# RWKV attention feeding a dense block: a shorter first block, own terms as TensorE products, idle products only in planned gaps

## The chip, the cores and the metric

One core of one Trainium2 chip. The metric is device time in microseconds (us). Kernels that are compared were run in turn on the same chip, together with the kernel before; the experiments ran in groups on chips 1, 4 and 8, so across groups the ratios are compared and not the medians. A kernel on one core has no second core to show a slow die; every profiled run quoted here was classed as fast (one unprofiled run of e5_kw_after_rT was slow). A run's time is about 1.7 us longer than its profiled span (640.26 against 638.5 in the changed kernel).

Short names: PE is TensorE (matmul), DVE is VectorE, ACT is ScalarE, POOL is GpSimd, SP is the engine that issues the loads.

## The reference, cut to what matters

```python
# r, k, v: (4, 8, 768, 48); w, u: (8, 48)
for t in range(S):
    cur = einsum('bhd,bhe->bhde', u * kt, vt)            # the "own term" of step t
    y[:, :, t] = einsum('bhd,bhde->bhe', rt, state + cur)
    state = w * state + einsum('bhd,bhe->bhde', kt, vt)
x = y.transpose(0, 2, 1, 3).reshape(B * S, H * D)        # (3072, 384)
h = x @ w_in                                             # (3072, 2048)
return (h - tanh(h)) @ w_out                             # (3072, 384)
```

## The kernel before

The attention works in 24 units of 64 steps of two batches. Within a unit the decay is taken out by scaling: r times powers of w, k times inverse powers, so that the step-by-step recurrence becomes matmuls ("levels", "outputs", "state"). Sixteen units come early, 8 later. The dense block turns finished units (two make one block x transposed, tile `xt`) into h, g and o; its weights arrive as 64-bit words in 16 pieces and are converted by five DVE and two ACT instructions each.

The kernel does not write its instructions in a fixed order. It adds tasks with an engine, an estimated cost and predecessors to a plan, and a list scheduler puts them in an order for each engine. The chip then runs each engine's queue in that order, so an instruction that waits holds up everything behind it (a case of 4.34 us is shown below).

```python
IDLE = 80
...
    def turn_over():                                    # one pair of idle products
        for i in range(2):
            T.matmul(idle[:, 0, :128], ident, ident, start=True, stop=True)
    kept = [add("PE", .25, turn_over, due=2e9) for _ in range(IDLE)]
...
    # unit n (early: n < 16)
        def own():
            t.rk = work.tile([128, H, D], F32, name="rk", tag="rk")
            E.tensor_tensor(t.rk, rt[:, :, :D], t.kt, ALU.mult)         # r*k
        def own_sum():
            t.du = work.tile([128, H], F32, name="du", tag="du")
            V.tensor_reduce(t.du, t.rk, axis=mybir.AxisListType.X, op=ALU.add)
        def diagonal(hs):                                               # onto the diagonal
            ...
            A.mul(t.at[:, h % 2, h // 2], same, t.du[:, h : h + 1])
...
        x.turn = add("PE", .46, lambda: turn(rt), [x.r, ..., tabs, downs, flagged])
        x.rT = add("DVE", .62, scale_r, [x.turn, ups])
        x.kw = add(e, cost, lambda: E.tensor_tensor(kw[:, :, :D], t.kt, w_down, ALU.mult), [x.k, downs, b2.out])
        turn_k = add("PE", .46, lambda: turn(kw), [x.kw, x.rT])
        x.kT = add("ACT", .5, copy_k, [turn_k])
        x.rk = add(e, cost, own, [x.r, x.k, b2.du, b1.rk])
        now = add(e, cost, lambda: E.tensor_tensor(t.rk, t.rk, ub, ALU.mult), [x.rk, bonus])
        x.du = add("DVE", .47, own_sum, [now, b2.diag])
        ...
        x.lev = add("PE", ..., levels, [x.kT, x.rT] + ...)
        x.cp = add("DVE", .64, lambda: V.copy_predicated(t.at, before, lev), [x.lev, x.diag])
        x.out = add("PE", 1.3, outputs, [x.cp, x.v, b1.xt, b1.rest, b1.add])
...
    for t in plan.order():
        t.run()
```

## Time and profile before

| | before |
|---|---|
| time, median of the first three runs | 646.72 us (644.96 to 647.88) |
| span of the profiled run | 646.0 us |
| PE busy | 624.5 us (97%) |
| first h product of the dense block | 54.38 us in the chain, 54.31 in PE's timeline |
| idle products (identity times identity) | 160 |

The prediction shows the lines for the idle products, the chain and the stages. Three more rows are needed to compare with later. The span is cut into 40 slices of 16 us; each digit is the busy share in tenths (for PEclk the granted clock, for DMA the busy share of the transfer engines).

```profile
DVE  3558899999996755757656555555645555454552
PEclk9999999999999999999999999999999999999998
DMA  6957549676101001001113110100103100100101
```

The reader is to see that the clock never drops, and that the transfers have free room between 32 and 96 us (5, 7, 5, 4). The same for 30 to 90 us in one row (columns: stretch, length, busy time of PE, weight loads, DVE, ACT, POOL with counts; granted clock; DMA share; GB/s):

```profile
30.00:90.00 60.00, 54.79 (x934) 46.38 (x926) 48.37 (x80) 36.07 (x89) 18.71 (x24) 1.00 0.60 131
```

### The profile page before, as it was taken

The page shows a single profiled execution, that of the slowest core. Times are in us where ns is not written, and L with a number is a line of the kernel's source. Part 1 is how long each engine was busy: PE and PEld are TensorE (multiplying, and loading weights), DVE is VectorE, ACT ScalarE, POOL GpSimd, SP SyncE. Part 2 cuts the span into 40 slices and gives each one's busy share as a digit, 9 for nine tenths or more (in the row PEclk, how much of TensorE's full clock was granted, in tenths as well). Part 3 has the DMA queues.
Part 4 walks back from the last instruction along what each step waited for, and adds up shares of the span by engine and source line. Part 5 has one row for each costly group of instructions (what it writes and reads, how often), then busy time and mean ns, then how long its engine had stood idle before and what let it go on. Part 6 is the DMA issues. An engine that isn't in the chain of part 4 may idle for free.

```text
span 646.0 us, 13413 instructions
## 1 busy us (share of the span) xinstructions
PE 624.5 (97%) x5383; PEld 471.8 (73%) x5383; DVE 420.3 (65%) x659; ACT 375.4 (58%) x788; POOL 113.1 (18%) x145
## 2 busy tenths in 40 slices
PE   9999899999999999999999999999999999999995
PEld 8997676776777777777777777777776776776773
DVE  3558899999996755757656555555645555454552
ACT  1436678877976545545556545655545655654752
POOL 1032243326021102103102100210116203001000
PEclk9999999999999999999999999999999999999998
DMA  6957549676101001001113110100103100100101
GB/s 131 210 98 177 125 86 151 164 133 161 25 14 30 15 1 26 12 1 35 34 31 80 26 25 1 38 18 1 37 10 60 38 2 8 26 0 9 25 0 29
DMA packets 88163, 33.80 MB, mean 52 GB/s; under 512 B 78620, under 2 KB 82972, under 8 KB 88092
## 3 DMA queue, kind: packets, MB, share of 16 engines
q1 hardware_dynamic: 85788, 31.67, 24.0%
q0 software_dynamic: 2304, 1.18, 0.7%
q8 instruction: 44, 0.72, 0.5%
q14 instruction: 27, 0.22, 0.1%
HBM read 26.94 MB, written 4.72 MB: 49 GB/s over the span
## 4 chain that ended last, share of the span: by engine, by line
PE 83%; DVE 10%; DMA 2%; issue 2%; ACT 1%; POOL 0%; DVEq 0%; ACTq 0%; SPq 0%; POOLq 0%
PE o L199 35%; PE h L162 35%; PE h L386 6%; PE yk_ps L444 4%; PE x_ps L485 2%; DMA rt<-in_r_dram 1%; DVE g L192 1%; DMA kt<-in_k_dram 1%; DVE power L136 1%; PE x_ps L444 1%; DVE tg L188 1%; DVE g L186 1%; DVE tg L190 1%; DVE at L587 1%; DVE w_in_sb L137 1%
## 5 line engine op out<-in xcount | busy, mean ns | idle before, releaser
L199 PE MATMUL o<-w_out_sb,g 128*128 128x384 f32 x768 | 281.2, 490 | 6.0 <-DVE g L192 6.0
L162 PE MATMUL h<-xt,w_in_sb 128*128 128x256 f32 x1152 | 280.9, 381 | 0.0
L162 PEld LDWEIGHTS h<-xt,w_in_sb 128*128 128x128 f32 x1152 | 216.4, 190 | 62.5 <-issue 0.2
L199 PEld LDWEIGHTS o<-w_out_sb,g 128*128 128x128 f32 x768 | 141.9, 190 | 70.2 <-DVE g L192 9.0
L171 ACT ACTIVATE s<-h 128x512 f32<-128x512 f32 x96 | 57.3, 597 | 176.2 <-PE h L162 176.1
L188 DVE SCALAR_TENSOR_TENSOR tg<-s,tg 128x512 f32<-128x512 f32 x96 | 68.9, 718 | 117.0 <-ACT tg L175 117.0
L186 DVE TENSOR_TENSOR g<-h,th 128x512 f32<-128x512 f32 x96 | 65.5, 682 | 35.3 <-ACT tg L175 34.9
L192 DVE COPY_PREDICATED g<-small,tg 128x512 f32<-128x512 int32 x96 | 74.2, 772 | 7.9 <-DVE g L186 0.5
L190 DVE SCALAR_TENSOR_TENSOR tg<-q,tg 128x512 f32<-128x512 f32 x96 | 70.7, 736 | 6.0
L179 ACT ACTIVATE small<-s,smallb 128x512 f32<-128x512 f32 x96 | 70.3, 732 | 0.0
L177 ACT ACTIVATE q<-s,m1b 128x512 f32<-128x512 f32 x96 | 69.6, 725 | 0.0
L173 ACT ACTIVATE th<-h 128x512 f32<-128x512 f32 x96 | 57.4, 598 | 1.5 <-PE h L162 1.5
L175 ACT ACTIVATE tg<-h 128x512 f32<-128x512 f32 x96 | 57.1, 595 | 0.0
L592 POOL TENSOR_TENSOR state<-state,power 128x384 f32<-128x384 f32 x22 | 36.8, 1672 | 94.0 <-DVE state L570 64.6
L564 POOL DMA_DIRECT2D xt<-rest x72 | 36.9, 518 | 92.0 <-ACT rest L550 54.2
L386 PE MATMUL h<-ident 128*128 128x128 f32 x320 | 41.1, 289 | 2.7 <-POOL ident masks.py:199 1.5
L577 POOL TENSOR_TENSOR kw<-kt,w_down 128x384 f32<-128x384 f32 x8 | 9.1, 1139 | 192.5 <-PE yk_ps L444 192.5
L508 ACT ACTIVATE at<-same,du 128x64 f32<-128x64 f32 x128 | 33.9, 340 | 14.5 <-DVE du L501 14.4
L386 PEld LDWEIGHTS h<-ident 128*128 128x128 f32 x320 | 39.4, 203 | 3.0 <-POOL ident masks.py:199 1.5
L497 POOL TENSOR_TENSOR rk<-rt,kt 128x384 f32<-128x384 f32 x8 | 8.4, 1051 | 97.8 <-DMA rt<-in_r_dram 87.9
L587 DVE COPY_PREDICATED at<-before,x_ps 128x512 f32<-128x512 int32 x23 | 16.6, 721 | 10.8 <-PE x_ps L444 10.7
L444 PEld LDWEIGHTS yk_ps<-at,vt 64*64 64x64 f32 x768 | 13.4, 134 | 13.6 <-DVE at L587 8.2
(88 smaller groups left out, 427.3 us busy)
## 6 DMA issues: line engine op xcount, KB each, us to landing
st<-in_moe_w_out_dram SPq DMA_DIRECT2D x8, 768.0 KB, 5.2
rt<-in_r_dram SPq DMA_DIRECT2D x48, 96.0 KB, 3.2
kt<-in_k_dram SPq DMA_DIRECT2D x48, 96.0 KB, 3.3
vt<-in_v_dram SPq DMA_DIRECT2D x48, 96.0 KB, 3.2
st<-in_moe_w_in_dram SPq DMA_DIRECT2D x16, 288.0 KB, 5.6
out_dram<-part SPq DMA_DIRECT2D x24, 96.0 KB, 2.2
out_dram<-o SPq DMA_DIRECT2D x24, 96.0 KB, 2.2
st<-in_moe_w_in_dram SPq DMA_DIRECT2D x16, 96.0 KB, 5.3
```

What stands on the lines that cost most here:

```text
L162: self.nc.tensor.matmul(t.h2[:, z], self.w_in_sb[:, t.f // 2, kk, z * 128 : (z + 1) * 128], self.xts[t.j][:, kk].rearrange("p b t -> p (b ...
L171: A.activation(out, t.h, AF.Square)
L173: A.activation(out, t.h, AF.Tanh)
L175: A.activation(out, t.h, AF.Tanh, scale=G1)
L177: A.activation(out, t.s, AF.Square, bias=self.m1b)
L179: A.activation(out, t.s, AF.Relu, bias=self.smallb, scale=-1.0)
L186: V.tensor_tensor(t.g, t.h, t.th, ALU.subtract)
L188: V.scalar_tensor_tensor(t.tg, t.s, C4, t.tg, ALU.mult, ALU.mult)
L190: V.scalar_tensor_tensor(t.tg, t.q, K1, t.tg, ALU.add, ALU.mult)
L192: V.copy_predicated(t.g, t.small.bitcast(I32), t.tg)
L199: self.nc.tensor.matmul(self.outs[i], t.g2[:, z, i * C : (i + 1) * C], self.w_out_sb[:, t.f + z, :], start=t.first and z == 0, stop=t.last ...
L386: T.matmul(idle[:, 0, :128], ident, ident, start=True, stop=True)
```

## The change

Three intentions:

1. The first two units ("direct") turn the raw keys as soon as they land and scale them afterwards by the transposed table, so that nothing waits for the table's way back; their part of `xt` is written without the small fills by DMA.
2. For 8 units, the own terms (sum over d of r·u·k) are computed as a second set of small TensorE products whose diagonal is copied out, instead of DVE's product, product with u, and sum.
3. Idle products are no longer a fixed 80 pairs: the plan puts one in for each 0.18 us of planned PE idle time, until the first h product.

Smaller parts of the change were never tested alone. For the 8 units the decay of the state moves from POOL to ACT, and the first two state copies move from DVE to ACT. The plan gets start times for the engines and other transfer costs: a weight piece counted 768 x 1024 bytes at 230e3 bytes per us, 3.42 us, and now counts 2.5 us.

Core of the diff (cut; memory for the new tiles, the moved state work and the final checks are left out):

```diff
+OWN = 8
-IDLE = 80
...
-    kept = [add("PE", .25, turn_over, due=2e9) for _ in range(IDLE)]
+    plan.fill = "PE", .18, lambda: T.matmul(idle, ident, ident, start=True, stop=True)
...  (in the scheduler)
+            if filling and t.engine == self.fill[0]:
+                for i in range(int((start - free[t.engine]) / self.fill[1])):
+                    done.append(SimpleNamespace(..., run=self.fill[2]))
+                filling = t is not self.fill_until
...  (weight pieces: the plan's transfer cost)
-        of = [add("SP", .55, step, [free], data=weights.COLS * 1024 / len(weights.piece(n)[1]))
+        of = [add("SP", .55, step, [free], data=2.5 / len(weights.piece(n)[1])) for _ in weights.piece(n)[1]]
...
+        early, product = n < L * (FIRST + 2), n < OWN
+        direct = j == 0
...
+        if direct:
+            own_rs = add("ACT", .5, own_r, [x.turn])
+            x.rk = add("PE", .46, lambda: turn(t.kt, x_banks[n == 1][:, :, :256]), [x.k])
+            own_ks = add("ACT", 1.1, lambda: own_k(x_banks[n == 1][:, :, :256], u_col), [x.rk, keeps])
+            x.kT = add("DVE", .62, scale_k, [x.rk, doubled])
+        else:
+            now = add("PE", .46, lambda: turn(kw), [x.kw, x.rT])
+            x.kT = add("ACT", .5, copy_k, [now])
+            own_rs = x.rT
+            if product:
+                own_ks = add("ACT", 1.1, lambda: own_k(turned, w_u), [now, w_us])
+        if product:
+            x.own = add("PE", .7, own_levels, [own_rs, own_ks, x.rT, x.kT])
+            x.diag = add("DVE", .64, lambda: V.copy_predicated(t.at, same..., own_lev), [x.own, b2.out])
+        else:                                            # as before: rk, times u, sum, diagonal
...
-        x.cp = add("DVE", .64, lambda: V.copy_predicated(t.at, before, lev), [x.lev, x.diag])
+        x.cp = add("DVE", .64, lambda: V.copy_predicated(t.at, before, lev), [x.lev, b2.out] + ([] if product else [x.diag]))
```

## The prediction

> **What bounds the kernel now.** I read the page first: TensorE (PE) is busy for 97% of the span. What it is busy with shows in the costliest groups (columns: line, engine, operation, tiles, shapes, count | busy us, mean ns of one | idle time before and its releaser).
>
> ```profile
> PE 624.5 (97%) x5383; PEld 471.8 (73%) x5383; DVE 420.3 (65%) x659; ACT 375.4 (58%) x788; POOL 113.1 (18%) x145
> ...
> L199 PE MATMUL o<-w_out_sb,g 128*128 128x384 f32 x768 | 281.2, 490 | 6.0 <-DVE g L192 6.0
> L162 PE MATMUL h<-xt,w_in_sb 128*128 128x256 f32 x1152 | 280.9, 381 | 0.0
> ...
> L386 PE MATMUL h<-ident 128*128 128x128 f32 x320 | 41.1, 289 | 2.7 <-POOL ident masks.py:199 1.5 <-issue 1.2
> ```
>
> The reader is to see the last line: 320 records of identity times identity, 160 idle products (two records each), whose result nobody reads. Next, the chain of work that ended last, limited to the first 60 us (start, us, what):
>
> ```profile
> 1.53 8.71 PE h L386 x52
> 10.23 0.15 PE x_ps L391
> 10.38 7.79 PE h L386 x68
> 18.17 0.44 PE x_ps L379 x4
> ...
> 31.66 1.17 issue
> ...
> 35.85 3.32 PE h L386 x28
> 39.17 0.44 PE x_ps L485 x4
> 39.61 3.13 PE h L386 x28
> ...
> 48.38 4.02 PE h L386 x36
> ...
> 54.38 2.79 PE h L162 x12
> ```
>
> The idle products ARE the chain. Added up in this view they take 39.8 us of the 52.9 us between 1.53 and 54.38, where the first real h product (L162) starts; the useful PE work in between is 11.9 us and the one wait 1.17 us. They were planned at 0.25 us a pair, and 68 records (34 products) take 7.79 us: 0.229 us each, 0.46 us a pair. So 80 pairs planned as 20 us of filler became nearly twice that, in an engine that runs its orders in sequence.
>
> Last, the busy time by stretch (stretch, length, then busy time with counts of PE, PEld, DVE, ACT, POOL; clock; DMA share; GB/s):
>
> ```profile
> 0.00:52.00 52.00, 49.31 (x673) 47.99 (x674) 27.13 (x57) 17.38 (x49) 8.52 (x28) 1.00 0.72 146
> 52.00:100.00 48.00, 43.61 (x718) 33.93 (x717) 42.94 (x72) 36.31 (x90) 14.53 (x17) 1.00 0.63 133
> 100.00:150.00 50.00, 45.48 (x736) 32.96 (x738) 48.47 (x78) 39.04 (x90) 19.24 (x23) 1.00 0.79 148
> 150.00:200.00 50.00, 49.40 (x375) 37.47 (x365) 49.17 (x78) 38.58 (x80) 9.83 (x4) 1.00 0.18 49
> 200.00:300.00 100.00, 100.00 (x691) 73.62 (x691) 64.57 (x99) 57.97 (x118) 17.76 (x23) 1.00 0.10 19
> ```
>
> Three stages: to 52 us PE turns idle products while VectorE (DVE) has 25 us free; from 52 to 200 us DVE is full (weight conversion, dense elementwise work, attention units) and PE loses 9.5 us; from 200 us PE alone is full. Whatever the start saves passes to the end only if DVE and the DMA can follow through the middle stage.
>
> **What the Trainium skill says.** (1) "TensorE: Matmul & The Clock Gate", Part 1: the PE array runs at half clock until about 3.4 us of sustained work, and falls back after an idle window of that size. The trace agrees at the start: the first 16 records fill 3.47 us (217 ns each), later ones need 115 ns, and the change comes near 7 us. This is why idle products exist, and why the 16 first ones that remain will be slow. (2) "FP8 and Floating Point Precision", TensorE Precision Notes: true FP32 takes four passes. An estimate from it and the 2.4 GHz of the first page: 4 x 128 / 2.4 = 213 ns; the trace has 229. So 0.18 us, the new planning cost of one idle product, is still too short. (3) "TensorEngine Tiling (Array Packing)", 64x64 Mode: four independent tiles. The trace agrees: 16 such products (32 records, x_ps<-rT,kT) take 0.62 us in the chain, 0.04 us each, so own terms by products are cheap. (4) "DMA: Bandwidth & Descriptors", Specifications: line rate wants at least 512 B per transfer. Here 78620 of 88163 packets are smaller, and from 10 to 15 us the DMA share is 0.98 at only 190 GB/s. The start is near this limit.
>
> **The change part by part.** I counted instructions in the order of the changed program, engine by engine.
>
> *Idle products*: 160 become 49 (groups of 16, 6, 4, 7, 3, 3, 3, 7), all ahead of the first h. The first 16 are cold: about 25 records by 7 us, the remaining 7 at 0.115, so they end near 7.8 us (6.3 us). The other 33 at 0.229 cost 7.6. Sum 13.9 instead of 39.8: 25.9 us less.
>
> *First block*: the raw keys are transposed as soon as they land and scaled afterwards by the table, so that turning does not wait for the table's way back. I walk the chain with durations of the trace. Decay column on PE 7.8 to 8.0; clamp 0.43, scan 0.70, reciprocal 1.78 on DVE to about 11.1; scaled r (0.69), doubled table 0.41, scaled k 0.69 to about 13.4; own products and levels of unit 0 on PE to 14.6; DVE has bounds, one weight step (0.55) and two predicated copies (0.74 each) to about 16.1; outputs, transpose and state products to 18.0. Unit 1 runs through DVE behind this: k, two kw, r, the two copies, to 21.6; outputs to 23; ACT copies xt and k of unit 2 to 24.1; state and level products to 25.7. Beside it the conversion of weight piece 0 ends on DVE at about 26. So the first h starts at about 26.5 us, against 54.4. The other check: 1.5 us start, 13.9 idle, 10.4 useful on PE add up to 25.8. The direct units leave out the little fills of xt by DMA; those were beside other work already.
>
> But this is not 28 us of gain. At its first h the old kernel had more units behind it: 11.9 us of useful work against 10.4, of which some is new.
>
> *Own terms of 8 units*: PE gains 16 products per unit, 0.57 us each time: 4.6 us, plus 0.5 us for the extra thirds in the two direct units. This lies on PE, the bound of the late stage: a sure cost of 5.1 us. DVE loses three steps of 0.47 (product, times u, sum) and gains one copy of 0.63: 0.78 x 8 = 6.2 less. With two k scalings (+1.2) and two state copies moved to ACT (-0.9) DVE is 5.9 us lighter. ACT loses 8 small scalings (2.12 us per unit, as four take 1.06) and gains 4 scalings of k (about 1.3) and 4 of the state decay (about 1.2, off POOL): even.
>
> **The sum.** Useful PE work before: 646.0 - 39.8 idle - 2.7 start - 9.5 gaps to 200 us - 1.7 later gaps - 7.7 tail = 584.6. After: 584.6 + 5.1 = 589.7, plus 13.9 idle, 1.5 start, and if gaps and tail stay as they are (18.9): 624.0. Independently by DVE: before, DVE had done 163.5 us when its full stage ended near 195 us. After: 163.5 - 5.9 = 157.6, starting at 8.1 without a pause: 165.7, plus the share of gaps of the old full stage (4.4 in 135, here about 5) makes 171; the end moves by 24, to 623. Both roads agree. As denser work in three engines should lose a little more, I say 625.
>
> **Rivals.** (a) *DVE takes over as the bound*: 97 to 98% busy from 100 to 200 us speaks for it. In-order queues with PE, DVE and DMA all nearly full could leave DVE 8% idle instead of 3%: 12 us instead of 5, end near 631. Against it: the change itself takes 5.9 us off DVE. (b) *DMA becomes the bound*: by 160 us the DMA share adds up to 112 us; pressed into 137 us that is 82%, and the weights' 4 and the units' 3 buffers must hide the bursts. The old trace already has rt and kt landings of 5 to 7 us on the chain between 98 and 111 us. For the first h it is enough: three units and two pieces are 3.3 MB, some 20 us at 170 GB/s. A burst that holds up PE for 3.4 us would cost cold products too. That would give 632 to 638. (c) *The idle time was hidden*: had PE waited for data anyway, without fills it would wait as long and the time would be 646 + 5 = 651. Against it: in 0 to 52 us the chain shows no wait but 1.17, and DVE was waiting for PE transposes, not for data. (d) *Better than the sum*: with POOL off DVE's way and an accurate plan, half of the middle gaps vanish: 618.
>
> **Range and chances.** The saved 25.9 and the added 5.1 are nearly sure: 20.8 net. The rest is waits: 5 us fewer (d) to 11 more (a, b). Hence 625, range 616 to 636. Two per cent is 633.8; rivals (a) and (b) together reach beyond it about one time in eight. Faster 0.86, same 0.13, slower 0.01.
>
> **What would show it right or wrong.** Right: about 98 idle records with 14 us in the chain; the first h at 25 to 29 us; x_ps<-rT,kU (and rU,kU) groups near 0.6 us per unit; DVE near full from 9 us; PE full from about 172 us; the last 450 us unchanged. Wrong in the walk: a first h past 32 us, with DMA of st, kt or rt ahead of it in the chain. Wrong in the sum: PE gaps between 27 and 172 us well over 10 us, released by DVE at or g (rival a) or by DMA (rival b). A time above 640 would mean that the idle products had covered waits for data after all.

## The result, and the profile after

The changed kernel is correct and takes 638.88 us (median of 4 runs, 636.95 to 640.49) against 645.91 us of the kernel before in the same rounds. Ratios here are the mean time of one kernel's fast runs over the mean of the other's fast runs of the same rounds, so not quite the ratio of the medians: 0.9886, with a 95% interval of 0.9842 to 0.9929. That is 7 us faster and counts as "same" at the 2% line; 625 was predicted, with a range up to 636.

The page of the changed kernel, in the rows shown of before:

```profile
span 638.5 us, 13477 instructions
...
PE 609.5 (95%) x5449; PEld 452.9 (71%) x5449; DVE 416.5 (65%) x644; ACT 377.2 (59%) x789; POOL 92.8 (15%) x139
...
DVE  4796898999976766756666655455636655553651
PEclk9997999999999999999999999999999999999998
DMA  7989965782001001002113110200112100100101
```

The slices show at once what differs: the idle products' time is gone (PE 624.5 to 609.5 us busy), but the DMA digits are 8 and 9 from 16 to 80 us, and the clock drops to 7 in the fourth slice, where it was full before.

The chain of waits is no help for this profile: it breaks off at the last activation. So the first block is read from PE's timeline (start us, us, engine, line, operation, out<-in, shapes, count, and in brackets the idle time before with its releaser). First its idle products, then its own terms, then the first h:

```profile
1.53 5.42 PE L400 MATMUL h<-ident 128*128 128x128 f32 x32 [1.53 <-POOL ident masks.py:199]
...
13.25 0.70 PE L460 MATMUL x_ps<-rU,kU 48*64 48x64 f32 x32 [0.21 <-DVE kT L512]
...
27.84 0.48 PE L162 MATMUL h<-xt,w_in_sb 128*128 128x256 f32 x1
```

And the idle products in the costliest groups (busy us, mean ns of one, idle before):

```profile
L400 PE MATMUL h<-ident 128*128 128x128 f32 x98 | 14.3, 303 | 1.5 <-POOL ident masks.py:199 1.5
```

All of this is as predicted: 98 idle records, the first h at 27.84 us (26.5 said; 54.31 before), own products of 32 small matmuls in 0.6 to 0.7 us. The stages, with the edges of the prediction's table:

```profile
0.00:52.00 52.00, 43.75 (x950) 37.82 (x951) 40.09 (x73) 30.65 (x74) 8.65 (x33) 1.00 0.89 166
52.00:100.00 48.00, 41.46 (x654) 30.67 (x653) 37.14 (x62) 33.14 (x86) 5.75 (x12) 0.89 0.85 163
100.00:150.00 50.00, 46.85 (x727) 34.93 (x726) 49.43 (x77) 38.67 (x84) 12.31 (x16) 1.00 0.66 134
150.00:200.00 50.00, 48.54 (x310) 35.93 (x309) 42.84 (x68) 36.78 (x80) 4.36 (x3) 1.00 0.06 11
200.00:300.00 100.00, 100.00 (x635) 73.79 (x634) 65.30 (x98) 57.24 (x116) 18.17 (x23) 1.00 0.10 19
```

Up to 52 us PE is now idle for 8.2 us (before 2.7), from 52 to 100 us for 6.5 (before 4.4) at a clock of 0.89 (before 1.00). DVE, which was to be full from 9 us on, does 37.1 us of work in the 48 us from 52 to 100, less than before (42.9). DVE waits too, so it is not simply the bound. The same 30 to 90 us as above:

```profile
30.00:90.00 60.00, 50.91 (x945) 38.98 (x942) 49.97 (x80) 41.54 (x103) 5.90 (x12) 0.94 0.97 186
```

The DMA share went from 0.60 to 0.97. The largest wait lies there. PE's timeline, then DVE's, then the load's issue on SP:

```profile
40.62 0.69 PE L460 MATMUL yk_ps<-at,vt 64*64 64x64 f32 x32 [1.85 <-DVE at L655]
...
50.12 0.69 PE L460 MATMUL yk_ps<-at,vt 64*64 64x64 f32 x32 [2.03 <-DVE at L655]
...
57.49 1.11 PE L504 MATMUL x_ps<-ident,kw 128*128 128x128 f32 x4 [4.34 <-DVE rT L508]
```

```profile
56.28 0.56 DVE L631 TENSOR_TENSOR kw<-kt,w_down 128x384 f32<-128x384 f32 x1 [4.68 <-DMA kt<-in_k_dram]
56.75 0.68 DVE L508 TENSOR_TENSOR rT<-x_ps,w_up 128x512 f32<-128x512 f32 x1
```

```profile
47.64 2.96 SPq L492 DMA_DIRECT2D kt<-in_k_dram  x2
```

To be read from right to left: the keys of unit 6 are issued at 47.64 us and are there at 56.28. Their scaling (`kw`) stands at the head of DVE's queue; behind it stands `rT` of unit 5, whose input had been ready since 51.9. PE's next instruction waits for `rT`, and so PE stands for 4.34 us. In stretches of 1 us the granted clock is then 0.54 at 56 and 0.50 from 57 to 62 us:

```profile
56.00:57.00 1.00, 0.00 (x0) 0.00 (x0) 0.72 (x2) 0.00 (x0) 0.00 (x0) 0.54 1.03 313
57.00:58.00 1.00, 0.51 (x3) 0.51 (x4) 0.78 (x2) 0.00 (x0) 0.00 (x0) 0.50 1.10 289
...
61.00:62.00 1.00, 1.00 (x4) 0.81 (x3) 0.96 (x2) 0.80 (x3) 0.00 (x0) 0.50 1.21 227
```

**A ledger.** To compare the kernels, I split each profiled span into five parts: PE's waits up to 210 us (1 minus busy time, summed over stretches of 1 us, the start included); time lost at half clock (busy time times 1 minus the granted clock, same stretches); waits after 210 us with the tail; idle products; and the rest, which is useful PE work. For the idle products of before I use the 39.8 us of the prediction; for after, start to start in the timeline, 13.3 us.

| us | before | prediction's terms | after | after against prediction |
|---|---|---|---|---|
| waits to 210 us, with the start | 12.2 | 11.0 (1.5 + 9.5) | 19.4 | +8.4 |
| lost at half clock | 0.0 | 0 | 4.4 | +4.4 |
| waits later, tail | 9.3 | 9.4 (1.7 + 7.7) | 9.6 | +0.2 |
| idle products | 39.8 | 13.9 | 13.3 | -0.6 |
| useful PE work | 584.7 | 589.7 | 591.8 | +2.1 |
| span | 646.0 | 624.0 | 638.5 | +14.5 |

So 26.5 us of idle products were saved, about as foreseen, and 7.1 us more useful work was done, 2 more than foreseen; but 11.6 us against the kernel before came back as waits and half clock ahead of 210 us. The experiments ask why.

The ledger is of one execution. The four runs of the changed kernel took 636.95 and 637.49 us at a mean granted clock of 0.994, and 640.26 (the profiled one) and 640.49 us at 0.988 and 0.990. The half clock in the ledger is thus likely at the upper end of what this kernel shows.

### The profile page after: what moved, and what is told of

Same layout as the page of the kernel before. It is cut to its first block, busy times and chain, and to the rows that moved or that the text cites. A ratio compares the mean times of both kernels' runs of the same rounds, so it can differ in the third digit from the quotient of the medians.

```text
span 638.5 us, 13477 instructions
## 1 busy us (share of the span) xinstructions
PE 609.5 (95%) x5449; PEld 452.9 (71%) x5449; DVE 416.5 (65%) x644; ACT 377.2 (59%) x789; POOL 92.8 (15%) x139
## 5 line engine op out<-in xcount | busy, mean ns | idle before, releaser
L199 PE MATMUL o<-w_out_sb,g 128*128 128x384 f32 x768 | 284.1, 494 | 5.1 <-DVE g L192 3.0
L614 POOL DMA_DIRECT2D xt<-rest x66 | 32.3, 496 | 153.6 <-ACT rest L596 82.1
L460 PE MATMUL yk_ps<-at,vt 64*64 64x64 f32 x752 | 16.4, 224 | 7.8 <-DVE at L655 5.3
L664 POOL TENSOR_TENSOR state<-state,power 128x384 f32<-128x384 f32 x14 | 17.1, 1219 | 45.4 <-DVE state L620 37.8
L460 PEld LDWEIGHTS yk_ps<-rT,state 48*64 48x64 f32 x704 | 16.8, 134 | 8.3 <-issue 7.0
L620 DVE TENSOR_TENSOR state<-yk_ps,state 128x384 f32<-128x384 f32 x20 | 11.0, 551 | 14.2 <-ACT rest L600 14.2
L460 PE MATMUL yk_ps<-rT,state 48*64 48x64 f32 x704 | 19.8, 223 | 0.0
```

What stands on the lines that cost most here:

```text
L199: self.nc.tensor.matmul(self.outs[i], t.g2[:, z, i * C : (i + 1) * C], self.w_out_sb[:, t.f + z, :], start=t.first and z == 0, stop=t.last ...
L460: T.matmul(*args, skip_group_check=True, **how)
```

## The experiments

Sixteen kernels ran. All numbers in one table (ratio: to the kernel before of the same rounds; waits, half clock and DMA share from the profiled run, as in the ledger). "Wrong" means wrong on purpose, unless the table says otherwise. The interval of the changed kernel alone is 0.0044 to either side; with that of the other kernel, a difference from it of less than about 0.005 to 0.006 (3 to 4 us) is not shown.

| kernel | result | median us (runs) | ratio, 95% | span | first h | waits to 210 | half clock | DMA share 30-90 |
|---|---|---|---|---|---|---|---|---|
| before | correct | 645.91 (4) | 1 | 646.0 | 54.3 | 12.2 | 0.0 | 0.60 |
| after | correct | 638.88 (4) | 0.9886 [0.9842, 0.9929] | 638.5 | 27.8 | 19.4 | 4.4 | 0.97 |
| e1_idle48 | correct | 648.75 (13) | 1.0043 [1.0023, 1.0062] | 645.8 | 43.4 | 22.9 | 9.9 | 0.85 |
| e2_half_loads | wrong | 635.35 (4) | 0.9823 [0.9797, 0.9850] | 634.3 | 28.9 | 15.7 | 3.4 | 0.72 |
| e2b_half_loads_before | wrong | 645.47 (12) | 0.9985 [0.9968, 1.0002] | 642.9 | 52.0 | 10.0 | 0.0 | 0.44 |
| e4_hold2 | correct | 648.95 (15) | 1.0040 [1.0020, 1.0059] | 647.2 | 29.5 | 23.8 | 8.0 | 0.58 |
| e5_kw_after_rT | correct | 643.98 (20, one slow) | 0.9955 [0.9931, 0.9979] | 647.0 | 28.7 | 24.6 | 7.4 | 0.93 |
| e6_warm | wrong, not meant | 640.34 (4) | 0.9918 [0.9889, 0.9946] | 638.0 | 28.6 | 14.0 | 0.0 | 0.97 |
| e9_light_warm | correct | 639.30 (4) | 0.9893 [0.9848, 0.9938] | 636.5 | 28.0 | 14.3 | 1.7 | 0.94 |
| e7_less_dve | wrong | 636.74 (4) | 0.9866 [0.9825, 0.9907] | 634.6 | 30.1 | 15.7 | 3.3 | 0.93 |
| e7b_less_dve_before | wrong | 642.39 (9) | 0.9948 [0.9932, 0.9963] | 640.1 | 51.7 | 7.2 | 0.0 | 0.64 |
| e8_less_dve_half_loads | wrong | 633.17 (4) | 0.9792 [0.9759, 0.9824] | 633.4 | 31.1 | 13.3 | 6.3 | 0.75 |
| e10_reliefs_warm | wrong | 631.56 (4) | 0.9782 [0.9746, 0.9818] | 629.8 | 30.4 | 10.5 | 0.0 | 0.70 |
| e3_own2 | correct | 641.98 (11) | 0.9937 [0.9915, 0.9959] | 640.5 | 26.8 | 18.7 | 4.8 | 0.84 |
| e11_plan30 | correct | 642.35 (6) | 0.9909 [0.9875, 0.9944] | 644.5 | 28.3 | 20.1 | 9.7 | 0.90 |
| e12_plan35 | correct | 643.58 (17) | 0.9952 [0.9934, 0.9971] | 642.8 | 27.7 | 17.2 | 4.9 | 0.96 |
| e13_plan40 | correct | 638.13 (4) | 0.9862 [0.9824, 0.9901] | 636.9 | 27.3 | 17.6 | 3.2 | 0.91 |
| e14_fill23 | correct | 637.97 (4) | 0.9864 [0.9829, 0.9899] | 636.0 | 27.5 | 18.1 | 5.0 | 0.92 |

The four columns on the right, and the span, are of the profiled run alone. For some kernels that run lay well above the median: 648.70 us for e5_kw_after_rT (its 19 fast runs reach from 640.54 to 649.42), 646.18 for e11_plan30, 635.07 for e8_less_dve_half_loads. Differences of a few us in these columns can be those of one execution.

A profiled run can lie some us from the median (e5_kw_after_rT: its 20 runs fall into two groups, about 641 to 644 and 646 to 650, and the profile shows one of the second). Differences between a kernel and the changed one are worked out below from the two ratios times 646 us; where their intervals overlap, the difference is not called shown.

### Idle products alone: e1_idle48

```diff
 (the kernel before)
-IDLE = 80
+IDLE = 24
```

> The kernel before with 48 idle products instead of 160, nothing else changed (24 pairs instead of 80). Theory A (the start was idle products, and behind it the transfers become the bound: the first 90 us of the changed kernel run at a DMA share near 1): the first h comes near 30 us, the DMA share rises to near 1 until 90 us, and the time is 636 to 642, so most of the change's 7 us come from the idle products alone. Rival B (the new first block is what brings the gain): the first h stays later than 35 us and the time is above 642. Rival C (the own products and their two serial copies cost the rest): without them this kernel reaches 622 to 630.

Measured: 1.0043, a little slower than before. The first h starts at 43.41 us, 11 us earlier, and nothing of it arrives at the end. The stages from 20 to 50 us:

```profile
20.00:30.00 10.00, 5.26 (x204) 4.34 (x204) 8.79 (x15) 5.65 (x15) 3.73 (x6) 0.98 0.98 155
30.00:40.00 10.00, 6.94 (x136) 5.89 (x136) 8.18 (x14) 6.40 (x22) 1.60 (x3) 0.50 0.98 253
40.00:50.00 10.00, 9.34 (x147) 7.92 (x148) 8.05 (x12) 4.86 (x9) 2.40 (x4) 0.67 0.91 161
```

PE is idle for 4.7 us of the ten from 20 to 30, and the ten after that run at half clock. What follows: in the kernel before, the 112 idle products covered waits and kept the clock up (waits up to 210 us rise from 12.2 to 22.9 us, half clock from 0 to 9.9). Fewer idle products alone are thus worth nothing. That it is the shorter first block that makes them unnecessary follows by elimination; it was not tested alone. In its pure form rival (c) of the prediction is confirmed for the old program and refuted for the new one, whose time did fall.

### Less to transfer: e2_half_loads and e2b_half_loads_before

```diff
+                hs = slice(0, 4 if n >= (5 if name == "k" else 3) else H)
-                Q.dma_start(out=(...)[HALF[z], :, :D], in_=src[half * 2 + z, :, steps_at, :]...)
+                Q.dma_start(out=(...)[HALF[z], hs, :D], in_=src[half * 2 + z, hs, steps_at, :]...)
```

From unit 3 (keys: unit 5) on, only 4 of 8 heads are loaded, so the result is wrong on purpose; the keys lie in three fixed tiles. The first is this edit on the changed kernel, the second on the kernel before.

> The changed kernel, instruction order identical, but from unit 3 on (k from unit 5) each load of r, k and v brings 4 of the 8 heads, the others keep stale data: a wrong result on purpose, with half the packets of these loads. Theory A: no wait of DVE for kt near 52 us, no half clock after it, the PE idle time before 200 us falls from 19 to about 12 us, time 622 to 630. Rival C (DVE and the own products' chain): the same waits of PE for DVE at, time 635 to 640.

> The kernel before with half of the r, k and v loads from units 3 and 5 on (wrong result on purpose). If the waits for transfers came into being with the change, as its first 90 us run at a DMA share near 1 and those of the kernel before do not: no gain, 644 to 648. If they were there already: 640 to 643.

Measured: 0.9823 on the changed kernel, 4.1 us less than its 0.9886 (intervals just overlapping, spans 634.3 against 638.5), short of the 622 to 630 that theory A expected; 0.9985 on the kernel before, whose interval holds 1. The 4.68 us wait for keys is gone, and from 50 to 60 us PE does 8.86 us instead of 5.54:

```profile
50.00:60.00 10.00, 8.86 (x144) 6.96 (x148) 8.95 (x15) 6.07 (x16) 0.00 (x0) 0.83 0.83 231
```

What follows: these loads did not measurably hold the old kernel, and they hold the new one by about 4 us. That is not all that transfers may cost, for the weights' loads stay whole (the DMA share from 30 to 90 us is still 0.72). Half clock (0.83) appears even without that wait. Transfers are one of the causes; that they are the whole cause is not shown.

### Less for DVE: e7_less_dve and e7b_less_dve_before

```diff
-        yield V.scalar_tensor_tensor(power, hi, 0x80000000, power, ALU.bitwise_and, ALU.bitwise_or)
-        yield V.tensor_tensor(dst, dst, power.bitcast(F32), ALU.mult)
+        yield
+        yield
```

Two of the five DVE steps of each weight conversion are left out, wrong on purpose. DVE's busy time falls by 25.2 us (416.5 to 391.3) in the changed kernel and by 23.5 us in the kernel before; 28 had been expected.

> The changed kernel, order identical, without the last two of the five DVE steps of each weight conversion (wrong result on purpose): about 28 us less work on DVE, all before 180 us. Theory G (DVE, whose queue is full from 100 to 180 us and which PE waits for before that, is the bound of the first 180 us): the waits for at, part and g shrink, time 620 to 629. If transfers and the clock alone hold the start back: the wait for kt near 52 us and the half clock stay, time 632 to 638.

> The kernel before without the last two DVE steps of each weight conversion (wrong result on purpose). If DVE held its first 200 us by more than chains of latency: 636 to 641 (PE waits before 200 us fall from 12.2 to under 6 us). If not: 643 to 647.

Measured: 0.9866 on the changed kernel (1.3 us less than without the edit by the ratios, not shown, and 3.9 by the spans) and 0.9948 on the kernel before (3.4 us less, shown). So DVE held the old kernel somewhat already, and holds the new one hardly more. Some 25 us of DVE work are worth 1 to 4 us, where theory G expected 620 to 629 us: DVE's load is not the bound in the sense of rival (a).

### Both: e8_less_dve_half_loads

The two edits above together on the changed kernel.

> Both reliefs at once: two DVE steps less per weight piece and half of the r, k and v loads from units 3 and 5 on (wrong result on purpose). If DVE and transfers together hold the start back, nothing but PE is left: 590 us of useful PE work, 13 us of idle products, 1.5 us of start, some 8 us of tail and a few waits, 613 to 620. If something else does (the order itself, chains of latency): above 625.

Measured: 0.9792, 6.1 us less than the changed kernel, with intervals apart. At 633.17 us it is above the 625 from which the expectation reckoned with something else (the order, chains of latency). In the profiled run, the slowest of four, waits fall to 13.3, but half clock costs 6.3 us: waits of 1 to 2 us in the thinner stretches suffice for it.

### Keeping the clock up: e6_warm and e9_light_warm

```diff
+        def keep_warm(count):
+            for _ in range(count):
+                put(yk_ps[:, 1, 448:], ident, ident[:, :64], start=True, stop=True)    # e6; e9: start=False, stop=False
         def outputs():
+            keep_warm({3: 6, 4: 8, 7: 8}.get(n, 0))                                    # e9: {3: 5, 4: 4, 7: 6}
...
+            def turn_k():
+                keep_warm(14 if n == 5 else 0)                                         # e9: 10
+                turn(kw)
```

Small idle products stand in PE's queue exactly where the changed kernel waits.

> The changed kernel with 36 small idle products (64 columns, into an unused part of a PSUM bank) at four places where PE waited about 2 us or more: ahead of the outputs of units 3, 4 and 7 and ahead of turning the keys of unit 5. Theory F (the freed PE time became waits, and the waits let the clock fall to half, 56 to 63 us and 94 to 97 us in the changed kernel's trace, at a cost of about 4.3 us there): no stretch at clock 0.50 before 200 us, the waits themselves shorter only by the fills, time 633 to 636. Rival (the clock costs nothing because DVE is late anyway): 637 to 640.

> The changed kernel, correct result, with 25 small idle products (about 0.22 us each in the run before, written without clearing flags this time): 5, 4 and 6 ahead of the outputs of units 3, 4 and 7 and 10 ahead of turning the keys of unit 5, everywhere less than the wait seen there, so that they should lie wholly inside waits. Theory F (half clock costs): no half clock before 100 us and 2 to 4 us less than the changed kernel, 634 to 637. Rival (the next wait takes it back): 637.5 to 640, waits longer elsewhere.

Measured: in the profiled runs the clock is 1.00 up to the tail in e6_warm and nearly so in e9_light_warm (1.7 us lost), and neither kernel is faster: 0.9918 and 0.9893 against 0.9886. The waits before 210 us fall by 5 us, but the 36 and 25 products themselves take longer than that (8.9 us busy in e6_warm, 50 records and 6.2 us in e9_light_warm). The result of e6_warm is wrong by 0.10, which was not meant. The likely reason is that its start flag hit sums that were still pending in the same bank: with the flag off, and fewer products, e9_light_warm is correct. What follows: in these executions half clock is a consequence of the waits, since it goes when they are filled. Where a wait is filled, its time is used up all the same. What a full clock is worth stays open. In e9_light_warm's profile 2.7 us of half clock and 5.1 us of waits go, 6.2 us of products come, and the span is 2.0 us shorter, which is within the noise. Nor did the fills hold the clock in every run: the mean granted clock of e9_light_warm's four runs is 0.997, 0.995, 0.992 and 0.991, at 636.06, 638.24, 641.53 and 640.37 us; in e6_warm it is 0.990 to 0.997, without such an order.

### The upper end: e10_reliefs_warm

Both reliefs of e8_less_dve_half_loads and 16 light idle products (6, 4 and 6 ahead of the outputs of units 3, 4 and 7).

> Less DVE work, half the loads, and light fills ahead of the outputs of units 3, 4 and 7 (wrong result on purpose). The run without fills had 13.3 us of PE waits and 6.3 us lost at half clock in the first 200 us. If waits for transfers and DVE and the half clock are all that lies between the forecast 625 and the measured 639: 626 to 630. If something else is missing from the account: 632 or more.

Measured: 0.9782, 631.56 us, span 629.8. The time lies between the two expectations (626 to 630, or 632 and more). No half clock, waits of 10.5 us up to 210 us. That is about what the prediction assumed (11.0). Its 16 products are busy for 4.1 us; without them the span would be 625.7 (an estimate: 629.8 - 4.1), where the prediction's sum of 624.0 with the 2.1 us of larger useful work gives 626.1. PE's row of 30 to 60 us shows it:

```profile
30.00:40.00 10.00, 9.78 (x170) 7.95 (x171) 7.40 (x13) 6.90 (x17) 0.00 (x0) 1.00 0.84 185
40.00:50.00 10.00, 9.37 (x253) 7.65 (x253) 7.85 (x13) 9.30 (x23) 3.01 (x6) 1.00 1.01 181
50.00:60.00 10.00, 9.34 (x162) 7.46 (x163) 7.83 (x14) 7.11 (x17) 0.00 (x0) 1.00 0.77 217
```

What follows: the sum closes once its assumption on the waits is made true, so no large term besides waits and half clock is missing. But that took 25 us less on DVE, half of the attention's loads and idle products, all at once. What the idle products add to the two reliefs is not shown (0.9782 against 0.9792).

### Loads out of the way, order kept: e4_hold2

```diff
+    for n in range(4, 8):                  # weight pieces 4 to 7 wait for units 6 to 9
+        for x in sends[n]:
+            for y in (units[n + HOLD].turn, units[n + HOLD].kw):      # HOLD = 2
+                x.after.append(y); y.then.append(x); x.open += 1
```

Four weight pieces are loaded later, so that the units' loads have the transfer engines to themselves; correct.

> The changed kernel with a correct result, where the loads of weight pieces 4 to 7 (the second quarter) are planned behind the first steps of units 6 to 9 instead of between the loads of units 5 to 7. Theory A: r, k and v of units 5 to 8 land some 8 us earlier, the 4.7 us wait for kt and the half clock vanish, time 626 to 633. Rival D (DVE is the true bound of the first 180 us): conversion work moved later is missed later, time 637 to 645.

Measured: 1.0040, about 10 us slower than the changed kernel, and a little slower than before the change. The share of transfers from 30 to 90 us is 0.58, about as in the old kernel (0.60). Now weights come late:

```profile
80.00:90.00 10.00, 5.78 (x115) 4.57 (x113) 5.56 (x10) 8.38 (x25) 0.00 (x0) 0.95 0.61 117
...
140.00:150.00 10.00, 4.77 (x15) 2.53 (x14) 10.00 (x15) 5.62 (x12) 5.28 (x7) 0.85 0.93 168
```

From 140 to 150 us DVE is full, with late conversions among its work, the transfers are full again, and PE is half empty. The waits that the trace names there are PE's for the small fills of `xt` by DMA:

```profile
PE h L163 <- DMA xt<-rest: 5.2, 3, 2.4
```

These are 5.2 us in three waits, the longest 2.4, up to 210 us; the changed kernel has none of this kind. So work that was put off is missing, or in the way, later. Which of the two, late conversions or crowded fills, costs more was not tested.

### Another order on DVE: e5_kw_after_rT

```diff
-        x.kw = add(e, cost, lambda: ..., [x.k, downs, b2.out])
+        x.kw = add(e, cost, lambda: ..., [x.k, downs, b2.out] + ([b1.rT] if early else []))
```

This takes away the collision of the trace: `kw` of unit 6 can no longer stand ahead of `rT` of unit 5. It does so for all 16 early units, and the plan orders everything anew around it, so it is not that one collision alone that changes; correct.

> The changed kernel with one order changed: the scaling of k of unit n+1 comes behind the scaling of r of unit n on DVE, so that a late kt no longer holds up an rT that is ready. Theory A in its narrow form (one late transfer at the head of an in-order queue): the 4.3 us wait of PE and the half clock vanish, time 629 to 634. Theory A in its wide form (transfers as a whole are too slow to 90 us): the wait moves elsewhere, time 635 to 640.

Measured: 0.9955, slower than the changed kernel by 4.5 us. In the profiled run, one of the slower ones, the wait moved instead of going: in its groups PE's transposes of `kw` wait 7.2 us for DVE's `rT`, and DVE waits 6.5 us for a weight piece to land. That agrees with the line of 4.34 us being only the place where the delay shows. This was the story that the trace had suggested most strongly. In its narrow form, which expected 629 to 634 us from this edit, it falls.

### The plan's idea of transfers: e11_plan30, e12_plan35, e13_plan40

The plan counts 2.5 us of transfer per weight piece (3.42 before the change). An estimate from the trace of the changed kernel says more: the DMA share of 0.92 over 0 to 90 us is 82.8 us; loads worth 11 units at 4.0 us (0.08 of 50 us between 250 and 300 us, where one unit is loaded alone) take 44, ub about 1, and 11 pieces share the rest, 3.4 us each.

```diff
-        of = [add("SP", .55, step, [free], data=2.5 / len(weights.piece(n)[1])) ...]
+        of = [add("SP", .55, step, [free], data=3.5 / len(weights.piece(n)[1])) ...]     # 3.0 and 4.0 likewise
```

> The changed kernel, but the plan counts 3.0 us of transfer for a weight piece instead of 2.5. Theory P (the order is at fault): waits before 210 us fall from 19.4 to about 15, half-clock loss below 4.4, time 632 to 636. Theory Q (the resources are full): 637 to 641.

> As the one before with 3.5 us, nearest to the 3.4 that the trace lets one estimate. Theory P: best of the three, 628 to 634, no wait over 2 us of VectorE for the keys' load at the head of its queue between 45 and 60 us. Theory Q: 637 to 643, the same waits at other places; the plan's own end moves from 620.3 to 628.2, 8 us later, which speaks for Q.

> As the one before with 4.0 us, above the estimate. Theory P: between the two before or a little worse than 3.5, 630 to 637. Theory Q: 637 to 645.

Measured: 0.9909, 0.9952, 0.9862. With the cost nearest to the trace the time is worse (by 4.3 us), with 4.0 it is within the interval of the changed kernel. In e12_plan35 no wait of DVE for keys is left between 45 and 60 us, and PE has waits of another kind there instead (later it also waits 4.3 us for the fills of `xt`, between 119 and 143 us):

```profile
34.51 0.82 PE L460 MATMUL yk_ps<-at,vt 64*64 64x64 f32 x32 [1.62 <-DVE at L655]
...
44.59 0.69 PE L460 MATMUL yk_ps<-at,vt 64*64 64x64 f32 x32 [1.71 <-DVE at L646]
...
56.75 0.69 PE L460 MATMUL yk_ps<-at,vt 64*64 64x64 f32 x32 [1.69 <-DVE at L646]
```

Such a wait is the stretch from the level products over two predicated copies on DVE (0.72 us each) to the outputs. Whether PE has dense work to put there depends on what has been loaded and converted. What follows: theory P falls as it was stated, for no better transfer cost brought the times that it expected (e13_plan40, with 638.13 us, comes within 1.1 us of them). Orders do differ, by some 11 us between e4_hold2 and the best; but eight correct orders with nearly the same work (after and e4, e5, e9, e11 to e14) all have waits of 14.3 to 24.6 us and half clock of 1.7 to 9.7 in their profiled runs. It agrees with theory Q, that this stage has no slack, without proving it: a much better order may exist.

### Fewer idle products still: e14_fill23

```diff
-    plan.fill = "PE", .18, ...
+    plan.fill = "PE", .23, ...
```

> The changed kernel, but an idle product is planned with 0.23 us, which it takes warm, instead of 0.18: 38 products instead of 49, nothing else differs. If the 49 lie in gaps that the chain of the first block leaves anyway: 638 to 640, first h within 0.5 us of 27.8. If they hold up the first block: first h 1 to 2.5 us earlier and 636 to 638; if the 11 missing ones let the clock fall: a part below 1.00 before 28 us.

Measured: 0.9864, 637.97 us; 38 products instead of 49; the first h 0.4 us earlier, and no clock below 1.00 before 30 us. 1.4 us by the ratios, well inside the intervals: the 11 products left out had cost nothing that shows. With e13_plan40 it has the lowest median of the correct kernels, but neither is shown to beat the changed kernel.

### Own terms by products or by DVE: e3_own2

```diff
-OWN = 8
+OWN = 2
```

Units 2 to 7 compute their own terms on DVE again, as before, and their state decay goes back to POOL; correct.

> The changed kernel with own terms as products only in the two units of the first block, units 2 to 7 as before (rk, sum and scaled diagonals): 6 x 0.57 = 3.4 us less on PE, 6 x 0.78 = 4.7 us more on DVE. Theory G: DVE is what counts, so slower, 641 to 646. Rival C (the products and their two serial copies cost): faster, 630 to 636.

Measured: 0.9937, 3.3 us slower than the changed kernel (the intervals just overlap; spans 640.5 and 638.5). The sum had booked these six units' products as 6 x 0.57 = 3.4 us of sure cost on PE, against 6 x 0.78 = 4.7 us off DVE. The kernel is more likely to gain by the products than to lose. If so, time on DVE (and the decay's place) counts for more in this stage than the sum, which booked PE's cost alone, says.

## Why the prediction was wrong

**Right: the removed work, with some luck.** 49 idle products where 49 were counted, 13.3 us where 13.9 was worked out. The first products ran slow, as the first of the prediction's points on the clock said, but only 16 records of 213 ns, up to 4.90 us; in the kernel before there were 26, up to 7.03 us, and the prediction took 25. Counted from 1.53 us these are 3.4 and 5.5 us: the "about 3.4 us" of that point fits the changed kernel, and not the kernel before, of whose trace the prediction said that it agrees. (The granted clock reads 1.00 in both stretches, so the ledger's half clock does not count them.) So the first 16 products took 5.36 us, from 1.53 us to the next instruction at 6.89, where 6.3 was worked out. First h at 27.84 us, inside 25 to 29: the decay column came 0.9 us early by this, and the walk from there to the first h took 21.0 us where 18.7 was said, so two errors partly cancel.

**Nearly right: the added work.** Useful PE work grew by 7.1 us instead of 5.1. The own products themselves are short, 0.5 to 0.7 us per unit as counted. Where the other 2 us lie was not looked for; the way of counting (overlapping ends, stretches of 1 us) may hold part of it.

**Wrong: "if gaps and tail stay as they are (18.9)".** This is the step that failed. The tail and the late gaps stayed (9.6 us). The gaps up to 210 us did not: 19.4 us with the start instead of 11.0, and another 4.4 us at half clock, a term that the sum lacked altogether. Of 14.5 us between the sum and the profile these two make 12.8. The prediction carried the old kernel's gaps into a stage where 27 us less time is available for the same loads, conversions and chains. It had a number for it in hand ("pressed into 137 us that is 82%"), kept it for rival (b) and left it out of the sum. The mean hid the crowd: 0.97 from 30 to 90 us, 0.35 from 100 to 210.

**The independent road by DVE was not independent.** It assumed DVE "starting at 8.1 without a pause". From 50 to 60 us DVE worked 5.10 us and from 60 to 70 us 6.51:

```profile
50.00:60.00 10.00, 5.54 (x79) 3.99 (x80) 5.10 (x11) 3.61 (x9) 0.00 (x0) 0.80 1.07 234
60.00:70.00 10.00, 10.00 (x182) 7.58 (x182) 6.51 (x11) 8.19 (x18) 0.00 (x0) 0.85 0.93 171
```

Both roads left out transfers, so that they agreed proves little.

**The rivals.** (b) named the right ingredients and even the cold products behind a wait of more than 3.4 us (here 4.34), and its band of 632 to 638 ends 1 us below the result. But it gave transfers the whole role. Halving the units' loads returns 4 us. (a) gave DVE the whole role. Taking 25 us from DVE returns 1 to 4. Both together with 16 idle products return 7 in time, and 9 of the waits. (c) was told as all or nothing. e1_idle48 shows that 112 idle products of the old program did cover waits; only together with the rest of the change does their removal pay. The prediction's argument against (c), that the chain shows no wait up to 52 us but 1.17, could not decide: while idle products stand in PE's queue, no wait can show there. (d) did not occur.

**What stays open.** The waits are shared by transfers, DVE, the chain of each unit and the clock, and they replace each other: no single edit that kept the result correct made the kernel measurably faster. How the 12 us divide among them could not be given, and whether a quite different order (fewer units early, say) would avoid them was not tried. What is shown is that the gaps and the clock did not stay; that it took four things crowded into the same 60 us, as argued here, fits the runs but is not shown by any one of them.

## What to carry to other kernels

When a start gets shorter, do not carry the old gaps over: list what every engine and the transfers must have done by the end of the crowded stage, and divide by the time that is left, for that stage and not for the mean. A line that shows the largest wait is where a delay becomes visible; before mending it, take the suspected resource away (half the loads, wrong on purpose) and see how much comes back. In this kernel, removing idle products that covered waits brought nothing by itself (e1_idle48).

## What the Trainium skill lacked or had wrong

- "TensorE: Matmul & The Clock Gate" (table of Part 1; "Avoid throughput drops mid-kernel" asks for no idle gaps over about 3 us). That agrees with the 4.34 us wait, after which the clock was 0.50 up to 62 us. But shorter waits were enough in thin stretches: in the changed kernel 2.07 us before 92.73 us, with 0.50 from 94 to 97 us. On the other hand 1.85 us before 40.62 and 2.03 before 50.12 did nothing. The page says that the clock is decided in windows of about 3.4 us that run freely, and names short repeated idles as a second way to lose it; what share of a window may be idle is lacking. The traces give it roughly. From the clock of the 1 us stretches, the half clock lasts from 56.08 to 62.91 and from 93.63 to 97.04 us, twice and once 3.41 us; in the other traces too it comes, before the tail, in multiples of that. Cut into stretches of 3.41 us along these edges, PE was idle for 86% of 52.67 to 56.08 and 61% of 90.22 to 93.63, and half clock followed both. The wait before 40.62 made 49% of its stretch (39.02 to 42.43), and the one before 50.12 lay across an edge and made 34% and 25%: the clock stayed. In all 18 traces up to 200 us, cut in the same way, half clock followed all 14 stretches at full clock that were idle for 60% or more, 18 of 30 between 45 and 60%, and 3 of 930 below. So where the edges fall decides as well. That they fall elsewhere in each run would explain why the mean clock of one kernel's runs differs (0.988 to 0.994 in the changed kernel); this is argued, not shown.

```profile
92.73 0.69 PE L460 MATMUL yk_ps<-at,vt 64*64 64x64 f32 x32 [2.07 <-DVE at L646]
```

```profile
93.00:94.00 1.00, 1.00 (x64) 0.91 (x54) 1.00 (x3) 0.00 (x0) 0.00 (x0) 0.82 0.06 16
94.00:95.00 1.00, 1.00 (x5) 1.00 (x6) 1.00 (x3) 0.94 (x4) 0.00 (x0) 0.50 0.00 0
```

- No page says that idle products are not free replacements of waits: in one profiled run 25 of them removed 2.7 us of half clock and 5.1 us of waits and cost 6.2 us of busy time (e9_light_warm); over its runs no gain was measured (0.9893 against 0.9886).
- "PSUM — Partial Sum Buffer" (zero region): not lacking but worth its place, since the runs agree with it. Idle products with the start flag, written to unused columns of a bank with pending sums, came with a relative error of 0.10 (36 of them, e6_warm); with 25 at the same places and without the flag the result was correct (e9_light_warm).
- No page gives the landing time of loads in a crowd: keys in two loads of 96 KB, issued from 47.64 us on, were usable at 56.28, over 8 us later, at a DMA share of 0.93 to 1.42 in stretches of 1 us. From 47 to 57 us the medians from issue to landing were 6.2 us (keys), 6.9 (v) and 7.7 (r).
